# Loading q first and turning it one batch ahead in a fused attention and mixer kernel

## The chip, the core and the metric

The kernel runs on one core of a Trainium2 chip. A core has five engines that work side by side and wait for one another by semaphores: TensorE (PE; its weight loads, PEld, overlap its products), VectorE (DVE), ScalarE (ACT), GpSimd (POOL) and SyncE (SP). In this kernel SP only issues DMAs, and POOL issues the loads. Sixteen DMA engines move the data, and every queue shares them. The metric is device time of one execution in microseconds; lower is better.

## The reference

Eight batches go through an attention with a projected length of 64 for keys and values, and then through a mixer block. Cut to what is computed:

```python
k_proj = np.einsum('ks,bhsd->bhkd', E, k)      # 8 batches, 8 heads, S=1024, D=64, K=64
v_proj = np.einsum('ks,bhsd->bhkd', F, v)
attn = softmax(scale * q @ k_proj.T)           # over the 64 projected positions
x = (attn @ v_proj) as [8, 1024, 512]
h = np.maximum(x.T @ w_tok1, 0.0) @ w_tok2     # over the sequence, 1024 -> 256 -> 1024
u = x + h.T
out = u + np.maximum(u @ w_ch1, 0.0) @ w_ch2   # over the channels, 512 -> 1536 -> 512
```

Inputs and outputs are float32 in HBM. The kernel loads q, k, v and the weights as bf16 (the DMA converts), accumulates in float32 and stores float32.

## The kernel before

A batch has two halves. The **front** of batch b (`front`, L213) makes u: it projects k and v with `EFT` (`k_mm` L145, `v_mm` L150), turns the projected keys (`kt_step`), computes the scores of one head at a time (`score_step`, L177) and their exponentials (L182), multiplies by the projected v (`ou_step`, L190 to L197), and then does the two products over the sequence (L244, L256) and the sum u (L260). The **main part** of batch b is `up` (L388, 24 tiles of 4 products) and `down` (L441, a product of blocks in the manner of Strassen, with sums on DVE and POOL, and two stores of 512 KB for each half, L487 and L491).

The main part of batch b is interleaved with the front of batch b + 1 by hand. Both are generators that yield costs in microseconds; the loop at the end (L507 to L524) takes a step of the front whenever its due time has come. So each engine gets one fixed order of instructions, and an engine that waits holds up all that is behind it on that engine. Batch 0 has a front of its own, `front_first`, in pieces of two heads, sorted by a list `ev` of times written out by hand.

The scores need q with the head's dimension on the partitions. `load` (L82, issued by POOL) brings q, k and v of a batch as tiles `q_sb`, `k_sb` and `v_sb` of 1 MB. `turn_q` (L91, issued by SP) turns `q_sb` into `qT` with two crossbar transposes by DMA (L95), one for heads 0 to 3 and one for heads 4 to 7, 512 KB each. Each of these tiles has a single buffer. So the load of the next q waits until the turn of this q is done, the turn of the next q waits until the scores of this batch have read `qT`, and the next k and v wait for the projections of this batch. Batch 0 turns its q on PE instead.

In the kernel before, the turn of batch b is the first thing in front b, and the loads of batch b + 1 come behind the projections of front b, in the order k, v, q (`load_all`). On SP two other users stand in the same queue: the four crossbar transposes of u into `uT` at the end of a front (L262), which the next main part reads, and the stores of the output. On POOL the loads stand in one queue with three sums for each half of `down` (L475 to L477).

Of the kernel before, what the change touches and what calls it, by code (L numbers as in the profile page):

```python
# [16 lines left out]
def kernel(  # L17
# [15 lines left out]
    B, H, S, D = q.shape  # L33
# [52 lines left out]
    def load_all(b):  # L86
        load(b, "k", k)
        load(b, "v", v)
        load(b, "q", q)

    def turn_q(b):  # L91
        st["qT", b] = work.tile([P, H, 4, P], BF16, tag="qT", name="qT", bufs=1)
        for j in range(2):
            hs = slice(4 * j, 4 * j + 4)
            nc.sync.dma_start_transpose(  # L95
                out=st["qT", b][:, hs].rearrange("d h s p -> d (h s) p"),
                in_=st["q", b][:, hs].rearrange("p h x -> p (h x)"),
            )
# [24 lines left out]
    nc.gpsimd.dma_start(out=wt2, in_=moe_w_tok2.rearrange("(tc p) s -> p tc s", p=P))  # L123
    load_wc1(0)
    load_wc1(1)
    load_all(1)
    load_wc2(0)
    load_wc2(1)

# [74 lines left out]
    def new_front(b):  # L204
        st["x", b] = work.tile([P, SC, DM], BF16, tag="x_sb", name="x_sb", bufs=1)
        st["R", b] = work.tile([P, TC, DM], BF16, tag="R_sb", name="R_sb", bufs=1)
        st["u", b] = work.tile([P, SC, DM], BF16, tag="u_sb", name="u_sb", bufs=2)
        st["kp", b] = work.tile([KP, H, 2, D], BF16, tag="kprojs", name="kprojs", bufs=1)
# [4 lines left out]
    def front(b):  # L213

        al = slice(0, H)
        turn_q(b)
        new_front(b)
        kv_ps = front_ps("kv_ps")
        for si in range(SC):
            f = dict(start=(si == 0), stop=(si == SC - 1))  # L220
            k_mm(b, kv_ps, al, si, f)
            v_mm(b, kv_ps, al, si, f)
        k_out(b, kv_ps, al)
        if b + 1 < B:
            load_all(b + 1)
        yield 1.2
        v_out(b, kv_ps, al)
        yield 1.0
        kt_step(b, al, front_ps)
        yield 1.8  # L230
        score_step(b, 0, front_ps)
        yield 0.7
        score_step(b, 1, front_ps)
        yield 0.7
        for h in range(H):
            ou_step(b, h)
            yield 0.7
            if h + 2 < H:
                score_step(b, h + 2, front_ps)
                yield 0.5  # L240
        for t in range(TC):
            h_ps = front_ps("h_ps")
            for s in range(SC):
                nc.tensor.matmul(  # L244
                    h_ps, wt1[:, s, t * P : (t + 1) * P], st["x", b][:, s, :],
                    start=(s == 0), stop=(s == SC - 1),
                )
                if s % 2 == 1 and s < SC - 1:
                    yield 0.7
            nc.scalar.activation(out=st["R", b][:, t, :], in_=h_ps, func=ACT.Relu)  # L250
            yield 0.7 if t == 0 else 1.6
        new_uT(b)
        for s in range(SC):
            u_ps = front_ps("u_ps")
            for t in range(TC):
                nc.tensor.matmul(  # L256
                    u_ps, wt2[:, t, s::SC], st["R", b][:, t, :],
                    start=(t == 0), stop=(t == TC - 1),
                )
            nc.vector.tensor_add(out=st["u", b][:, s, :], in0=u_ps, in1=st["x", b][:, s, :])  # L260
            if s % 2 == 1:
                nc.sync.dma_start_transpose(  # L262
                    out=st["uT", b][:, s - 1 : s + 1].rearrange("d s c p -> d (s c) p"),
                    in_=st["u", b][:, s - 1 : s + 1].rearrange("p s d -> p (s d)"),
                )
            yield 0.9
# [7 lines left out]
    def front_first(fill):  # L274
        b = 0
        new_front(b)
        new_uT(b)
        st["qT", b] = work.tile([P, H, 4, P], BF16, tag="qT", name="qT", bufs=1)

        def q_turn(hp, psf):  # L280
            qt_ps = psf("qt_ps", BF16)
            for j in range(2):
                for s in range(4):
                    nc.tensor.transpose(
                        qt_ps[:, (j * 4 + s) * P : (j * 4 + s + 1) * P],
                        st["q", b][:, 2 * hp + j, s * P : (s + 1) * P], ident,
                    )
            nc.scalar.activation(
                out=st["qT", b][:, 2 * hp : 2 * hp + 2].rearrange("d h s p -> d (h s p)"),
                in_=qt_ps, func=ACT.Copy,  # L290
            )

        def proj(hp, psf, mm, fin):
            kv_ps = psf("kv_ps")
            hs = slice(2 * hp, 2 * hp + 2)
            for si in range(SC):
                mm(b, kv_ps, hs, si, dict(start=(si == 0), stop=(si == SC - 1)))
            fin(b, kv_ps, hs)

        def tok1(hp, psf):  # L300
            cs = slice(hp * P, (hp + 1) * P)
            h_ps = psf("h_ps")
            for t in range(TC):
                for s in range(SC):
                    nc.tensor.matmul(  # L305
                        h_ps[:, t * P : (t + 1) * P], wt1[:, s, t * P : (t + 1) * P],
                        st["x", b][:, s, cs], start=(s == 0), stop=(s == SC - 1),
                    )
            nc.scalar.activation(
                out=st["R", b][:, :, cs],  # L310
                in_=h_ps[:, 0 : TC * P].rearrange("p (t d) -> p t d", d=P), func=ACT.Relu,
            )

        def tok2(hp, psf, g):
            cs = slice(hp * P, (hp + 1) * P)
            u_ps = psf("u_ps")
            for i in range(4):
                for t in range(TC):
                    nc.tensor.matmul(
                        u_ps[:, i * P : (i + 1) * P], wt2[:, t, 4 * g + i :: SC],  # L320
                        st["R", b][:, t, cs], start=(t == 0), stop=(t == TC - 1),
                    )
            nc.vector.tensor_add(
                out=st["u", b][:, 4 * g : 4 * g + 4, cs],
                in0=u_ps.rearrange("p (s d) -> p s d", d=P),
                in1=st["x", b][:, 4 * g : 4 * g + 4, cs],
            )

        def turn_u(hp, psf):
            cs = slice(hp * P, (hp + 1) * P)  # L330
            ut_ps = psf("ut_ps", BF16)
            for s in range(SC):
                nc.tensor.transpose(ut_ps[:, s * P : (s + 1) * P], st["u", b][:, s, cs], ident)
            for g in range(2):
                o = st["uT", b][:, 4 * g : 4 * g + 4, hp, :]
                i_ = ut_ps[:, g * 512 : (g + 1) * 512].rearrange("d (s p) -> d s p", p=P)
                if g == 0:
                    nc.vector.tensor_copy(out=o, in_=i_)  # L338
                else:
                    nc.scalar.activation(out=o, in_=i_, func=ACT.Copy)  # L340

        ev = []
        t_q, t_k, t_v = (8.2, 12.0, 18.2, 21.9), (9.5, 13.2, 19.4, 23.1), (10.7, 14.4, 20.6, 24.4)
        t_w2 = 26.9
        for hp in range(HP):
            hs = slice(2 * hp, 2 * hp + 2)
            tk, tv, tq = t_k[hp], t_v[hp], t_q[hp]
            ev += [
                (tq, hp, lambda p, hp=hp: q_turn(hp, p)),
                (tk, hp, lambda p, hp=hp: proj(hp, p, k_mm, k_out)),  # L350
                (tk + 1.5, hp, lambda p, hs=hs: kt_step(b, hs, p)),
                (tv, hp, lambda p, hp=hp: proj(hp, p, v_mm, v_out)),
                (tk + 3.0, hp, lambda p, h=2 * hp: score_step(b, h, p)),
                (tk + 3.01, hp, lambda p, h=2 * hp + 1: score_step(b, h, p)),
            ]
            to = max(tv + 1.5, tk + 4.2)
            t1 = to + 2.6
            t2 = max(t1 + 1.7, t_w2 + 1.4 * hp)
            ev += [
                (to, hp, lambda p, h=2 * hp: ou_step(b, h)),  # L360
                (to + 1.1, hp, lambda p, h=2 * hp + 1: ou_step(b, h)),
                (t1, hp, lambda p, hp=hp: tok1(hp, p)),
                (t2, hp, lambda p, hp=hp: tok2(hp, p, 0)),
                (t2 + 0.5, hp, lambda p, hp=hp: tok2(hp, p, 1)),
                (t2 + 2.3, hp, lambda p, hp=hp: turn_u(hp, p)),
            ]
        ev += fill
        ev.sort(key=lambda e: e[0])
        pin = False
        for t, hp, fn in ev:  # L370
            pin = pin or hp is None
            fn(front_ps if pin else any_ps)
# [182 lines left out]
```

## Time and profile before

| | |
|---|---|
| median of three runs | 517.42 us (512.8 to 519.95) |
| the profiled execution | 514.69 us, of it span 512.9 us |
| granted TensorE clock, mean of the span | 0.953 |
| software DMA queue (loads) | 29.36 MB, 37.3% of 16 engines' span |
| hardware DMA queue (stores, crossbar) | 31.99 MB, 27.1% |

The profile is of one execution. Its page gives busy time for each engine, the span in 40 slices, the DMA queues, the chain of work that ended last, the costliest groups of instructions, and the DMA issues with their time from issue to landing. The trace behind it can be asked for waits, for a timeline, and for sums over stretches of time. An engine named with a q at its end, such as SPq, is the sequencer of that engine: it issues, waits and branches. The page's lines stand in the prediction where they are used.

### The profile page before, as it was taken

Reading aid. Unit: us, or ns where it says so; the run is one execution under the profiler, and the core shown is the slowest. Engines: PE = TensorE matmul, PEld = TensorE weight load, DVE = VectorE, ACT = ScalarE, POOL = GpSimd, SP = SyncE. Lnnn points to the kernel's source line nnn. Section 1 sums busy time; section 2 is a strip of 40 time slices with the busy share of each in tenths; the row PEclk is TensorE's granted clock in tenths of the full one; section 3 lists DMA queues with packets and bytes.
Section 4 is the critical chain, followed back from the end, with each engine's and each line's share of the span. In section 5 each row is a group of like instructions: output and inputs, shape, how many; then the busy total and the mean of one; then the engine's idle time right before and its main releaser. Section 6 shows DMA issues by size and latency. Waiting matters only on the chain.

```text
span 512.9 us, 7570 instructions
## 1 busy us (share of the span) xinstructions
PE 444.9 (87%) x3060; PEld 279.3 (54%) x3096; DVE 260.6 (51%) x527; ACT 187.1 (36%) x333; POOL 88.6 (17%) x95
## 2 busy tenths in 40 slices
PE   3789979975999759997699966999779999999996
PEld 2564356632486324863348633586335864487485
DVE  2374584553573525734457353474444747574453
ACT  3626731162502625025450263403544037502620
POOL 7320130300023000230002300024000220022022
PEclk9999989996999969998899997999879999999999
DMA  9999992897247981469914697056970661044003
GB/s 164 207 205 207 190 208 96 192 143 121 36 100 180 156 123 18 97 178 145 133 22 109 176 166 120 6 145 147 172 114 0 152 145 33 1 88 159 1 21 143
DMA packets 92690, 61.83 MB, mean 121 GB/s; under 512 B 59888, under 2 KB 88048, under 8 KB 92656
## 3 DMA queue, kind: packets, MB, share of 16 engines
q0 software_dynamic: 29200, 29.36, 37.3%
q1 hardware_dynamic: 63456, 31.99, 27.1%
q8 instruction: 24, 0.39, 0.3%
q14 instruction: 10, 0.08, 0.1%
HBM read 59.24 MB, written 16.78 MB: 148 GB/s over the span
## 4 chain that ended last, share of the span: by engine, by line
PE 67%; DMA 19%; DVE 7%; SPq 3%; ACT 2%; issue 1%; DVEq 0%; ACTq 0%
PE g_ps L388 22%; DMA qT<-q_sb 18%; PE be L441 12%; PE al L441 8%; PE ga L441 8%; PE h_ps L244 5%; PE u_ps L256 4%; DVE x_sb L197 4%; SPq L95 3%; PE ou_ps L190 3%; PE sco L177 2%; PE kv_ps L145 1%; DVE rdn L196 1%; DMA EF_f<-in_F_dram 1%; PE h_ps L305 1%
## 5 line engine op out<-in xcount | busy, mean ns | idle before, releaser
L388 PE MATMUL g_ps<-uT,wc 128*128 128x512 bf16 x768 | 198.5, 394 | 1.6 <-DVE uT L338 1.0
L420 ACT ACTIVATE g<-g_ps 128x512 bf16<-128x512 f32 x192 | 114.2, 597 | 132.7 <-PE g_ps L388 132.3
L388 PEld LDWEIGHTS <-wc 128*128 128x128 bf16 x768 | 74.4, 101 | 83.7 <-issue 16.0
L441 PEld LDWEIGHTS <-S 128*128 128x128 bf16 x768 | 75.3, 98 | 17.1 <-issue 0.3
L441 PEld LDWEIGHTS <-g 128*128 128x128 bf16 x576 | 56.6, 98 | 13.8 <-issue 0.3
L475 POOL TENSOR_TENSOR V<-V,u_sb 128x512 f32<-128x512 f32 x16 | 18.5, 1154 | 241.1 <-DVE V L470 241.1
L177 PE MATMUL sco<-qT,kbd 128*128 128x512 bf16 x48 | 20.8, 444 | 40.4 <-DMA qT<-q_sb 39.4
L182 ACT ACTIVATE attnT<-sco 128x512 bf16<-128x512 f32 x64 | 37.4, 594 | 47.4 <-PE sco L177 44.0
L190 PEld LDWEIGHTS <-attnT 128*128 128x128 bf16 x256 | 19.4, 103 | 62.6 <-issue 49.5
L196 DVE RECIPROCAL rdn<-ou_ps 128x8 f32<-128x8 f32 x64 | 13.2, 206 | 76.4 <-PE ou_ps L190 76.3
L441 PE MATMUL al<-wc,g 128*128 128x256 bf16 x384 | 50.4, 275 | 0.6
L441 PE MATMUL be<-dT,S 128*128 128x256 bf16 x384 | 48.8, 273 | 0.1
L197 DVE TENSOR_TENSOR x_sb<-ou_ps,rdn 128x512 bf16<-128x512 f32 x64 | 44.2, 691 | 2.2
L466 ACT ACTIVATE K<-al 128x512 f32<-128x512 f32 x16 | 9.6, 597 | 92.3 <-PE al L441 92.3
L260 DVE TENSOR_TENSOR u_sb<-u_ps,x_sb 128x512 bf16<-128x512 f32 x56 | 38.3, 685 | 6.6 <-PE u_ps L256 4.3
L406 DVE TENSOR_TENSOR S<-g 128x512 bf16<-128x512 bf16 x48 | 20.2, 421 | 31.5 <-ACT g L420 31.5
L190 PE MATMUL ou_ps<-vbd,attnT 128*128 128x130 bf16 x256 | 27.0, 232 | 9.6 <-DVE x_sb L197 7.4
L244 PE MATMUL h_ps<-x_sb,wt 128*128 128x512 bf16 x105 | 31.5, 379 | 1.7 <-DVE x_sb L197 1.3
L256 PE MATMUL u_ps<-R_sb,wt 128*128 128x512 bf16 x99 | 30.5, 379 | 0.0
L404 DVE TENSOR_TENSOR S<-g 128x512 bf16<-128x512 bf16 x48 | 20.2, 421 | 13.7 <-ACT g L420 13.5
L82 POOL DMA_DIRECT2D q_sb<-in_q_dram x11 | 9.2, 833 | 98.9 <-DMA qT<-q_sb 78.3
L441 PE MATMUL ga<-wc,S 128*128 128x256 bf16 x192 | 24.7, 273 | 0.0
(65 smaller groups left out, 395.5 us busy)
## 6 DMA issues: line engine op xcount, KB each, us to landing
out_dram<-o SPq DMA_DIRECT2D x32, 512.0 KB, 3.0
k_sb<-in_k_dram POOLq DMA_DIRECT2D x7, 1024.0 KB, 11.9
v_sb<-in_v_dram POOLq DMA_DIRECT2D x7, 1024.0 KB, 18.3
q_sb<-in_q_dram POOLq DMA_DIRECT2D x7, 1024.0 KB, 9.9
wc<-in_moe_w_ch_dram POOLq DMA_DIRECT2D x4, 384.0 KB, 13.9
wc<-in_moe_w_ch_dram POOLq DMA_DIRECT2D x2, 768.0 KB, 27.7
q_sb<-in_q_dram POOLq DMA_DIRECT2D x4, 256.0 KB, 8.7
k_sb<-in_k_dram POOLq DMA_DIRECT2D x4, 256.0 KB, 9.3
```

The source lines that it names most:

```text
L177: nc.tensor.matmul(sco, kbd[:, h, :], st["qT", b][:, h].rearrange("d s p -> d (s p)"), start=True, stop=True,)
L182: nc.scalar.activation(out=at, in_=sco, func=ACT.Exp, scale=scale)
L190: nc.tensor.matmul(ou[:, s // 2, o : o + 2 * D1], at[:, s * P : (s + 1) * P], vbd[:, h, :], start=True, stop=True,)
L197: nc.vector.tensor_tensor(out=st["x", b][:, :, h * D : (h + 1) * D].rearrange("p (b k) d -> p b k d", b=2), in0=ov[:, :, :, 0:D], in1=rdn[ ...
L244: nc.tensor.matmul(h_ps, wt1[:, s, t * P : (t + 1) * P], st["x", b][:, s, :], start=(s == 0), stop=(s == SC - 1),)
L256: nc.tensor.matmul(u_ps, wt2[:, t, s::SC], st["R", b][:, t, :], start=(t == 0), stop=(t == TC - 1),)
L260: nc.vector.tensor_add(out=st["u", b][:, s, :], in0=u_ps, in1=st["x", b][:, s, :])
L388: nc.tensor.matmul(st["g_ps", n], wc1[:, dc, cc * P : (cc + 1) * P], st["uT", b][:, 4 * sh : 4 * sh + 4, dc, :], start=(dc == 0), stop=(dc ...
L404: nc.vector.tensor_sub(out=s3, in0=a11, in1=a21)
L406: nc.vector.tensor_add(out=s1, in0=a21, in1=a22)
L420: nc.scalar.activation(out=o, in_=st["g_ps", n], func=ACT.Relu)
L441: nc.tensor.matmul(acc[:, e * HF : (e + 1) * HF], l[:, lc + c, l0 + (2 * j + e) * P : l0 + (2 * j + e + 1) * P], r[:, rc + c, r0 : r0 + HF ...
```

## The change

Two things move. First, the load of each q is issued ahead of the loads of its k and v. For batches 2 to 7 it stands at the beginning of the front of the batch before, ahead of that front's projections, while k and v stay behind them. Second, the turn of q of batch b + 1 is issued in front b, right behind the scores of head 7, and no longer at the beginning of front b + 1. For batch 1 it goes into `front_first`, behind the last scores of batch 0.

```diff
@@ the loads at the start
-    load_all(1)
+    load(1, "q", q)
+    load(1, "k", k)
+    load(1, "v", v)
...
@@ front(b)
-        turn_q(b)
         new_front(b)
+        if b + 1 < B:
+            load(b + 1, "q", q)
...
         k_out(b, kv_ps, al)
         if b + 1 < B:
-            load_all(b + 1)
+            load(b + 1, "k", k)
+            load(b + 1, "v", v)
...
             if h + 2 < H:
                 score_step(b, h + 2, front_ps)
+                if h + 2 == H - 1 and b + 1 < B:
+                    turn_q(b + 1)
                 yield 0.5
...
@@ front_first
+        ev.append((t_k[3] + 3.02, 3, lambda p: turn_q(1)))
         ev += fill
```

The order of the instructions on each engine shows it. PE, ACT and DVE have the same order in both kernels. Line numbers of the changed kernel are 6 or 7 higher behind the places of the edits.

SP before, from the turn of batch 1 to the first transposes of u of batch 2. The numbers tell buffers apart: `qT_704` and `qT_1177` are the turned q of batches 1 and 2, `uT_1038` and `uT_1527` those of u:

```order
L95 DMA_TRANSPOSE qT_704<-q_sb_111 128x16x128 x2
L487 DMA out_0_dram<-o1_823 128x1024
L491 DMA out_0_dram<-o2_824 128x1024
L262 DMA_TRANSPOSE uT_1038<-u_sb_709 128x8x128 x4
L487 DMA out_0_dram<-o1_1019 128x1024
L491 DMA out_0_dram<-o2_1020 128x1024
L95 DMA_TRANSPOSE qT_1177<-q_sb_734 128x16x128 x2
L262 DMA_TRANSPOSE uT_1527<-u_sb_1182 128x8x128 x3
```

SP in the changed kernel, the same stretch, where `qT_406`, `qT_929` and `qT_1398` belong to batches 1, 2 and 3:

```order
L95 DMA_TRANSPOSE qT_406<-q_sb_107 128x16x128 x2
L95 DMA_TRANSPOSE qT_929<-q_sb_711 128x16x128 x2
L494 DMA out_0_dram<-o1_823 128x1024
L498 DMA out_0_dram<-o2_824 128x1024
L268 DMA_TRANSPOSE uT_1041<-u_sb_709 128x8x128 x4
L494 DMA out_0_dram<-o1_1022 128x1024
L498 DMA out_0_dram<-o2_1023 128x1024
L95 DMA_TRANSPOSE qT_1398<-q_sb_1184 128x16x128 x2
L268 DMA_TRANSPOSE uT_1530<-u_sb_1182 128x8x128 x3
```

The turn of batch 2 moved ahead of two stores, of batch 1's four transposes of u, and of two more stores; each later turn moved likewise.

POOL before, from the loads of batch 1 to the sums of the first main part:

```order
L82 DMA k_sb_107<-in_k_dram 128x8x512
L82 DMA v_sb_109<-in_v_dram 128x8x512
L82 DMA q_sb_111<-in_q_dram 128x8x512
L113 DMA wc2_71<-in_moe_w_ch2_dram 128x6x512 x2
L82 DMA k_sb_730<-in_k_dram 128x8x512
L82 DMA v_sb_732<-in_v_dram 128x8x512
L82 DMA q_sb_734<-in_q_dram 128x8x512
L475 TENSOR_TENSOR V15_845<-V15_845,u_sb_138 128x512
```

POOL in the changed kernel, the same stretch:

```order
L82 DMA q_sb_107<-in_q_dram 128x8x512
L82 DMA k_sb_109<-in_k_dram 128x8x512
L82 DMA v_sb_111<-in_v_dram 128x8x512
L113 DMA wc2_71<-in_moe_w_ch2_dram 128x6x512 x2
L82 DMA q_sb_711<-in_q_dram 128x8x512
L82 DMA k_sb_732<-in_k_dram 128x8x512
L82 DMA v_sb_734<-in_v_dram 128x8x512
L482 TENSOR_TENSOR V15_845<-V15_845,u_sb_138 128x512
```

In each batch q stands ahead of k and v; the sums and the weights keep their places.

## The prediction

> **What bounds the kernel now.** I read the page first: the shares of the engines, the granted clock, the chain.
>
> ```profile
> span 512.9 us, 7570 instructions
> ...
> PE 444.9 (87%) x3060; PEld 279.3 (54%) x3096; DVE 260.6 (51%) x527; ACT 187.1 (36%) x333; POOL 88.6 (17%) x95
> ...
> PEclk9999989996999969998899997999879999999999
> ...
> PE g_ps L388 22%; DMA qT<-q_sb 18%; PE be L441 12%; PE al L441 8%; PE ga L441 8%; PE h_ps L244 5%; PE u_ps L256 4%; DVE x_sb L197 4%; SPq L95 3%; PE ou_ps L190 3%; PE sco L177 2%; PE kv_ps L145 1%; DVE rdn L196 1%; DMA EF_f<-in_F_dram 1%; PE h_ps L305 1%
> ```
>
> TensorE is busy 87% of the span, and the one thing beside it that holds a large share of the chain is the crossbar turn qT<-q_sb, 18%. The clock row has dips at places all over the span. The view of waits, PE alone (us in total, times, longest), says what PE stands still for:
>
> ```profile
> PE sco L177 <- DMA qT<-q_sb: 39.4, 7, 9.2
> PE e_ps L138 <- ACT EF_sb L134: 7.8, 1, 7.8
> ```
>
> Of the scores' waits for the turn there are seven, 39.4 us together; the next group is the single wait at the start. Whether these waits recur with the batches is read from the timeline of SP's queue (start, us spent issuing, line):
>
> ```profile
> 88.57 7.71 SPq L262 DMA_TRANSPOSE uT<-u_sb  x4
> ...
> 98.39 0.33 SPq L491 DMA_DIRECT2D out_dram<-o  x1
> ...
> 226.92 14.72 SPq L95 DMA_TRANSPOSE qT<-q_sb  x2
> ...
> 416.73 0.33 SPq L491 DMA_DIRECT2D out_dram<-o  x1
> 417.15 6.18 SPq L95 DMA_TRANSPOSE qT<-q_sb  x2
> 452.32 7.30 SPq L262 DMA_TRANSPOSE uT<-u_sb  x3
> ...
> 470.05 0.33 SPq L491 DMA_DIRECT2D out_dram<-o  x1
> ```
>
> The last store of a batch (L491) marks one period from the next. From 98.39 to 416.73 lie five periods, the fronts of batches 2 to 6: 318.34 us, 63.67 each. The sixth, front of batch 7, takes 470.05 - 416.73 = 53.32 us with the same instructions on PE, but without loads of k, v and q, for there is no batch 8. It is the pattern for a period in which the turn isn't disturbed. The windows compare the two, batch 3 and batch 7 from the start of the turn (us, busy per engine, granted clock, DMA share, GB/s):
>
> ```profile
> 162.74:176.00 13.26, 13.01 (x82) 5.87 (x81) 7.09 (x16) 9.76 (x18) 1.78 (x2) 1.00 1.11 190
> 176.00:184.86 8.86, 0.00 (x1) 0.00 (x0) 0.44 (x2) 0.60 (x1) 0.00 (x0) 0.67 1.10 148
> 184.86:190.00 5.14, 5.14 (x20) 2.32 (x20) 1.77 (x5) 2.13 (x4) 0.87 (x1) 0.58 0.59 74
> 417.15:430.41 13.26, 13.01 (x83) 5.88 (x81) 7.02 (x16) 9.77 (x18) 0.00 (x0) 1.00 0.67 131
> 380.00:512.90 132.90, 126.70 (x869) 83.07 (x876) 72.11 (x141) 46.68 (x82) 20.53 (x18) 1.00 0.29 77
> ```
>
> ```profile
> 184.86 0.59 PE L177 MATMUL sco<-qT,kbd 128*128 128x512 bf16 x1 [8.86 <-DMA qT<-q_sb]
> ...
> 430.32 0.38 PE L177 MATMUL sco<-qT,kbd 128*128 128x512 bf16 x1
> 435.29 0.10 PEld L177 LDWEIGHTS <-kbd 128*128 128x128 bf16 x1
> ```
>
> Up to the score of head 4 both take 13.26 us with PE busy 13.01: loads beside it don't slow PE. Then batch 3 waits 8.86 us for the second half of its turn, and batch 7 waits for nothing. Behind the wait the clock is 0.58 over 5.14 us in which PE is busy throughout, 5.14 x 0.42 = 2.2 us more. Why the turn is late is told by its landing (duration of the issue in ns; DMA to landing), in batch 3 and in batch 7:
>
> ```profile
> L95 SPq DMA_TRANSPOSE qT<-q_sb x1: 7935/7935/7935, 166.1 to 166.1; - x1
> DMA to landing us min/median/max: 18.7/18.7/18.7
> ...
> L95 SPq DMA_TRANSPOSE qT<-q_sb x1: 1967/1967/1967, 421.4 to 421.4; - x1
> DMA to landing us min/median/max: 4.4/4.4/4.4
> ```
>
> The same half of 512 KB takes 18.7 us beside the loads of k and v and 4.4 us alone.
>
> **The change part by part.** Nothing is added or removed: seven loads of q move ahead of k and v on POOL, and seven turns of two transposes each move to an earlier place on SP. PE, ACT and DVE keep their order.
>
> *The turn, batches 2 to 6.* It goes behind the last score of the batch before. In the pattern that score's weights load at 435.29, 18.1 us into the period, so SP issues about 18.7 in. It needs its q, and it would be slow if k and v were still coming:
>
> ```profile
> k_sb<-in_k_dram POOLq DMA_DIRECT2D x7, 1024.0 KB, 11.9
> v_sb<-in_v_dram POOLq DMA_DIRECT2D x7, 1024.0 KB, 18.3
> q_sb<-in_q_dram POOLq DMA_DIRECT2D x7, 1024.0 KB, 9.9
> ...
> 158.23 1.15 POOL L477 TENSOR_TENSOR K<-K,u_sb 128x512 f32<-128x512 f32 x1
> ...
> 165.37 0.91 POOL L82 DMA_DIRECT2D k_sb<-in_k_dram  x1 [5.99 <-PE kv_ps L150]
> ```
>
> The load of q has only to wait for POOL's add, whose end at 159.4 is 3.3 us ahead of the period's turn at 162.74; its own turn was done a period ago. At 9.9 us (the median, with nothing beside it but stores) it lands at 6.6. The loads of k and v are issued at 2.6 as before, and follow at 5.1 us each (the startup rows below), at about 17. So the turn at 18.7 finds q there and the DMA engines nearly free: issued within 6.2 us (row 417.15), landed 421.4 + 4.4 - 417.15 = 8.6 us later, at 27 of 53. The scores that need it come in the next period, more than 26 us on. Were the turn still disturbed, 18.7 us a half would also fit in. Price of the move: none; the five periods become like the sixth. That saves 318.34 - 5 x 53.32 = 51.7 us. Of it 39.4 are the waits, and the rest, 12.3 (2.5 a period), is the low clock behind them, as at 184.86.
>
> The Trainium skill (TensorE: Matmul & The Clock Gate, Part 1: The HAM clock gate) says that about 3.4 us of idle PE halves its clock, and about 3.4 us of activity restores it. By it one low window costs 1.7 us, so seven waits would cost at most 11.9 us, an estimate, and the sum would be 0.4 us higher. The trace has 1.00 where no wait lies, 380 to 512.9, so I keep the rows' 12.3.
>
> *What stands behind the turn on SP.* A turn that waits for a score or for q holds up what is queued behind it: the four transposes uT of the same batch and the two stores. In the pattern the first uT comes 452.32 - 417.15 = 35.2 us in and the turn leaves SP at 18.7 + 6.2 = 24.9; even the longest issue, 14.72 us at 226.92, ends at 33.4. Nothing waits: 0 us. Without that slack each microsecond would go to uT, and from there to the next batch's first products.
>
> *POOL.* If q has to wait for a turn, k and v now queue behind it. From batch 3 on it doesn't wait.
>
> *The startup, batch 1.* Here the loads form a backlog, and the turn falls into it:
>
> ```profile
> L82 POOL DMA_DIRECT2D k_sb<-in_k_dram x1: 884/884/884, 25.0 to 25.0; - x1
> DMA to landing us min/median/max: 15.0/15.0/15.0
> L82 POOL DMA_DIRECT2D v_sb<-in_v_dram x1: 873/873/873, 26.2 to 26.2; - x1
> DMA to landing us min/median/max: 18.9/18.9/18.9
> L113 POOL DMA_DIRECT2D wc<-in_moe_w_ch_dram x1: 826/826/826, 29.4 to 29.4; - x1
> DMA to landing us min/median/max: 29.4/29.4/29.4
> ...
> 54.92 0.40 PE L145 MATMUL kv_ps<-k_sb,EFT 128*64 128x512 bf16 x1
> ...
> 62.21 0.95 DVE L498 TENSOR_TENSOR dT<-wc,dT 128x1536 bf16<-128x1536 bf16 x1
> ...
> 68.44 0.15 PEld L177 LDWEIGHTS <-kbd 128*128 128x128 bf16 x1
> ```
>
> Loads landed in order, k at 40.0, v at 45.1, the last of wc2 at 58.8. Now q takes k's place and lands at 40.0, and the turn starts there. Beside a turn a load takes longer: v came 18.3 + 0.9 - 11.9 = 7.3 us behind k in the steady periods, against 5.1 here. So k lands by 47.3 and v by 54.6, just ahead of 54.92. The end of wc2 lies between 58.8 (no loss) and 58.8 + 5.1 = 63.9 (the turn's 1 MB at the pace of the loads); DVE reads it at 62.21, so it waits 0 to 1.7 us, and PE behind it. I take 0.9, the middle: both rows are equally near. The halves of the turn land by 40.0 + 18.7 = 58.7 and, the loads then ending, about 65, ahead of head 4 at 68.44. Load q of batch 2 waits for that, and k and v behind it come at about 82, needed at 98.8. Batch 2's turn, 5 us behind 68.44, meets them; by the 14.72 us of the longest issue SP is free at 88.1, and uT comes at 88.57.
>
> *Sum.* 512.9 - 51.7 + 0.9 = 462.1 us of span. The execution that was profiled took 514.69, 1.8 more than its span: 463.9 us. The median of the three runs, 517.42, stands 2.7 above that execution; the waits vary from run to run, so I expect the difference against the median to be somewhat larger.
>
> **The rivals.**
>
> *Only the waits go.* If the clock stays low for some other reason, 12.3 us stay: 476.2. Against it: 133 us at 1.00 in the window from 380 on, with PE busy 126.70. Chance 0.06.
>
> *The startup pays.* If the turn's second half lands behind 68.44, batch 1 gets the wait that batch 3 loses: 8.86 + 2.2 = 11.1 in place of 0.9, 474.1. For it: 18.7 us a half beside loads, two in a row from 40.0 would end at 77.4. Against it: the backlog ends by 63.9. The Trainium skill (DMA: Bandwidth & Descriptors, Queues, rings and completion order) has each DMA engine take the queues in turn, packet by packet, which is the rule against placing a turn in a backlog; 18.7 against 4.4 us agrees. Chance 0.06.
>
> *Slower.* The turn stands on SP ahead of the uT of its own front. Should q land more than 35.2 - 6.2 = 29 us into the period, each later microsecond is paid six times. To lose 2% over the 51.7 gained, q would have to be some 10 us later still, 42 us from issue: 463.9 + 6 x 10.3 = 526. Against it: 9.9 us to land, 18.3 at worst for v. Chance 0.02.
>
> *It does nothing.* The single buffers of q and qT chain load, turn and scores; if another such chain sets the period, the time stays at about 514. For it speaks no row; the sixth period shows none. Chance 0.03.
>
> **How the numbers follow.** The forecast has 0.83. Its low end is 0 for the startup and the 1.9 us by which the fastest run was below the profiled one: 461; I take 460. Its high end is 1.7 for the startup and the 5.3 us by which the slowest run was above it: 470.0; with half of the price of the startup's rival in, 472. The other cases, 0.17, stay outside. A measurement of this kernel tells about 2%, 10 us, from no change. Faster by more: the forecast and the first two rivals, 0.95; same 0.03; slower 0.02.
>
> **What would show it.** Right: no waits of the scores for the turn from batch 2 on; turns issued about 18.7 us into a period and landing within 9 us; periods of 53.3 us; clock 1.00 behind the startup. Wrong: SP still in a turn when u is ready, waits of up's products for uT, v of batch 1 behind 54.9, or a period above 55 with no idle PE.

## The result, and the profile after

| | before | changed |
|---|---|---|
| median of the runs | 517.53 us (4 runs, 512.8 to 519.95) | 472.71 us (4 runs, 471.46 to 473.26) |
| the profiled execution | 514.69 us, span 512.9 | 472.92 us, span 471.1 |
| granted TensorE clock | 0.953 | 0.984 |

The ratio is 0.914, with a 95% interval from 0.907 to 0.921. The kernel became faster by the mechanism that was forecast, but the time is 8.8 us above the forecast of 463.9, and 0.7 us above the range.

The changed kernel's page, span, TensorE, granted clock in 40 slices, and the chain:

```profile
span 471.1 us, 7571 instructions
...
PE 434.5 (92%) x3060; PEld 274.5 (58%) x3096; DVE 260.4 (55%) x527; ACT 186.3 (40%) x333; POOL 88.3 (19%) x95
...
PEclk9999989987999999999999999999999999999999
...
PE 85%; DVE 8%; DMA 3%; ACT 2%; issue 1%; SPq 0%; ACTq 0%; DVEq 0%
```

The chain is 85% TensorE, where the page before had 67%, and the transfers have 3% in place of 19%. The clock row is full from the eleventh slice on. The waits of TensorE in the changed kernel (us in total, times, longest):

```profile
PE e_ps L140 <- ACT EF_sb L136: 8.6, 1, 8.6
PE ou_ps L192 <- DVE x_sb L199: 7.4, 14, 2.2
PE g_ps L395 <- DMA uT<-u_sb: 6.7, 1, 6.7
```

All seven waits of the scores for the turn are gone. In their place stands one that the kernel before didn't have: a product of `up` waits 6.7 us, once, for a transpose uT. SP's timeline of the changed kernel tells in which period (start, us spent issuing, line):

```profile
74.73 12.77 SPq L95 DMA_TRANSPOSE qT<-q_sb  x2
...
99.22 0.33 SPq L498 DMA_DIRECT2D out_dram<-o  x1
127.88 4.15 SPq L95 DMA_TRANSPOSE qT<-q_sb  x2
...
162.02 0.47 SPq L498 DMA_DIRECT2D out_dram<-o  x1
181.13 4.55 SPq L95 DMA_TRANSPOSE qT<-q_sb  x2
...
428.28 0.33 SPq L498 DMA_DIRECT2D out_dram<-o  x1
```

From 162.02 to 428.28 lie five periods, the fronts of batches 3 to 7: 53.25 us each, and the forecast had 53.3. A turn is issued 181.13 - 162.02 = 19.1 us into its period (forecast 18.7), and the turns of batches 3 to 7 keep SP for 4.2 to 4.8 us each. But the period from 99.22 to 162.02, the front of batch 2, takes 62.80. That is 9.5 us more, and it is the whole difference from the forecast's span, 471.1 for 462.1. The windows of the changed kernel show how it divides (us, busy per engine, granted clock, DMA share, GB/s):

```profile
99.26:105.97 6.71, 0.00 (x1) 0.03 (x2) 0.00 (x0) 0.60 (x1) 0.00 (x0) 0.66 1.20 207
105.97:111.57 5.60, 5.60 (x21) 1.78 (x22) 0.00 (x0) 0.71 (x2) 0.00 (x0) 0.50 0.29 119
162.02:428.28 266.26, 261.48 (x1777) 162.73 (x1800) 156.76 (x315) 109.70 (x195) 43.73 (x41) 1.00 0.62 123
```

TensorE stands still for 6.71 us while the DMA engines are full, and then works 5.60 us at half the clock, 2.8 us lost. Two transposes, the third and the fourth of batch 1, have these landings in the changed kernel:

```profile
L268 SPq DMA_TRANSPOSE uT<-u_sb x1: 1231/1231/1231, 93.7 to 93.7; - x1
DMA to landing us min/median/max: 3.1/3.1/3.1
L268 SPq DMA_TRANSPOSE uT<-u_sb x1: 1320/1320/1320, 95.9 to 95.9; - x1
DMA to landing us min/median/max: 10.0/10.0/10.0
```

And POOL's timeline at that place:

```profile
93.36 1.16 POOL L484 TENSOR_TENSOR K<-K,u_sb 128x512 f32<-128x512 f32 x1
94.46 0.92 POOL L82 DMA_DIRECT2D q_sb<-in_q_dram  x1
111.68 0.87 POOL L82 DMA_DIRECT2D k_sb<-in_k_dram  x1 [16.30 <-PE kv_ps L152]
...
157.94 1.15 POOL L484 TENSOR_TENSOR K<-K,u_sb 128x512 f32<-128x512 f32 x1
159.03 0.91 POOL L82 DMA_DIRECT2D q_sb<-in_q_dram  x1
```

The load of q of batch 3 goes out at 94.46, as soon as POOL's last sum is done, and 1.4 us ahead of the issue of the fourth uT at 95.9. That transpose then lands in 10.0 us where its neighbour took 3.1. In the next period the load goes out at 159.03, and the last uT, issued at 153.0, has landed by then. Two causes are possible. Theory A: the load of q starves the last uT. Theory B: the turn of batch 2, which kept SP for 12.77 us from 74.73 on, beside the loads of k and v, has delayed the stores and uT behind it.

### The profile page after: what moved, and what is told of

Read it like the earlier page. It is cut to its first block, busy times and chain, and to the rows that moved or that the text cites. A ratio compares the mean times of both kernels' runs of the same rounds, so it can differ in the third digit from the quotient of the medians.

```text
span 471.1 us, 7571 instructions
## 1 busy us (share of the span) xinstructions
PE 434.5 (92%) x3060; PEld 274.5 (58%) x3096; DVE 260.4 (55%) x527; ACT 186.3 (40%) x333; POOL 88.3 (19%) x95
## 4 chain that ended last, share of the span: by engine, by line
PE 85%; DVE 8%; DMA 3%; ACT 2%; issue 1%; SPq 0%; ACTq 0%; DVEq 0%
PE g_ps L395 33%; PE be L448 13%; PE al L448 9%; PE ga L448 8%; PE h_ps L250 5%; PE u_ps L262 5%; DVE x_sb L199 4%; PE ou_ps L192 4%; PE kv_ps L147 3%; DMA uT<-u_sb 2%; PE sco L179 2%; DMA EF_f<-in_F_dram 1%; DVE rdn L198 1%; PE h_ps L311 1%; DVE u_sb L329 1%
## 5 line engine op out<-in xcount | busy, mean ns | idle before, releaser
L395 PE MATMUL g_ps<-uT,wc 128*128 128x512 bf16 x768 | 189.7, 381 | 8.3 <-DMA uT<-u_sb 6.7
L395 PEld LDWEIGHTS <-wc 128*128 128x128 bf16 x768 | 71.7, 98 | 85.5 <-issue 13.3
L192 PE MATMUL ou_ps<-vbd,attnT 128*128 128x130 bf16 x256 | 25.2, 221 | 10.0 <-DVE x_sb L199 7.4
L192 PEld LDWEIGHTS <-attnT 128*128 128x128 bf16 x256 | 17.4, 98 | 28.0 <-issue 14.2
L411 DVE TENSOR_TENSOR S<-g 128x512 bf16<-128x512 bf16 x48 | 20.2, 421 | 13.7 <-ACT g L427 13.5
L157 DVE CAST kprojs<-kv_ps 64x512 bf16<-64x512 f32 (+1 forms) x11 | 5.9, 536 | 39.2 <-ACT kprojs L156 39.2
L477 DVE TENSOR_TENSOR V<-ga,K 128x512 f32<-128x512 f32 x16 | 11.1, 691 | 25.7 <-PE ga L448 23.3
## 6 DMA issues: line engine op xcount, KB each, us to landing
q_sb<-in_q_dram POOLq DMA_DIRECT2D x7, 1024.0 KB, 13.5
```

The lines of the kernel that those rows point to most:

```text
L192: nc.tensor.matmul(ou[:, s // 2, o : o + 2 * D1], at[:, s * P : (s + 1) * P], vbd[:, h, :], start=True, stop=True,)
L395: nc.tensor.matmul(st["g_ps", n], wc1[:, dc, cc * P : (cc + 1) * P], st["uT", b][:, 4 * sh : 4 * sh + 4, dc, :], start=(dc == 0), stop=(dc ...
L411: nc.vector.tensor_sub(out=s3, in0=a11, in1=a21)
```

## The experiments

All are compared with the kernel before on the same chip. They ran on three chips, on which the kernel before had medians of 515.5 to 516.6 us, so times from different chips can differ by a microsecond for no other reason. A diff is against the changed kernel.

### e1 and e2: q behind the projections

```diff
 front(b)                                  # e1; e2 does it for b == 2 alone
-        if b + 1 < B:
-            load(b + 1, "q", q)
         kv_ps = front_ps("kv_ps")
...
         k_out(b, kv_ps, al)
         if b + 1 < B:
+            load(b + 1, "q", q)
             load(b + 1, "k", k)
```

> The load of q goes behind the projections of its front, still ahead of k and v; the turn stays early. Theory A (the load of q of batch 3 goes out 1.4 us ahead of the last transpose uT of batch 1 and starves it, which costs 6.7 us of wait and 2.8 us of low clock in one period): the wait of up's products for uT is gone, the period from 99 to 162 us becomes 53.3 like the others, the time is 472.7 - 9.5 = 463 us. Theory B (the turn of batch 2, kept on SP by the loads of k and v of batch 2 until 87.5 us, is what delays stores and uT): nothing changes there, 472 to 473 us.

> Only the load of q of batch 3 goes behind the projections of its front; all others stay as in the changed kernel. Theory A: 463 us, as much as when all are moved, since only this load meets a transpose of u. Theory B: 472 to 473 us.

Measured: 472.67 us (471.47 to 474.03, 6 runs) and 472.64 us (471.9 to 473.66, 6 runs). That looks like theory B, but the two kernels tell nothing. The line in the program moved behind the projections; the instruction on POOL did not. POOL does no part of the projections, so q stands on POOL in front of k as before, and nothing in front of it waits for TensorE. POOL's order is that of the changed kernel, row by row, and e1's timeline has the load at the old place:

```profile
93.13 1.17 POOL L483 TENSOR_TENSOR K<-K,u_sb 128x512 f32<-128x512 f32 x1
94.23 0.92 POOL L82 DMA_DIRECT2D q_sb<-in_q_dram  x1
```

They serve as two more measurements of the changed kernel: 472.6 to 472.7 three times.

### e3: the early turn alone

```diff
-    load(1, "q", q)
-    load(1, "k", k)
-    load(1, "v", v)
+    load_all(1)
 front(b)
-        if b + 1 < B:
-            load(b + 1, "q", q)
...
         if b + 1 < B:
-            load(b + 1, "k", k)
-            load(b + 1, "v", v)
+            load_all(b + 1)
```

> The turn is early as in the changed kernel, the loads have the order and the place of the kernel before (k, v, q). Theory A: q lands about 20 us into a period, some 1 to 2 us behind the last score, the turn is issued then, alone, and has left SP before uT; no load of q meets uT; 463 us. If q has to come first for the early turn to pay, the turn would come behind 35 us of a period and up's products would wait: above 475 us.

Measured: 462.18 us (461.64 to 462.54, 5 runs), ratio to the kernel before 0.896, interval 0.892 to 0.899. No wait of TensorE for a transpose by DMA is left. Loading q first is not needed for the early turn, and without it the kernel is 10.5 us faster than e1 and e2, which are the changed kernel on the same chip. Its median is the lowest of this study, though e4 and e5 lie within 1 us of it. It fits both theories: the load of q comes late here, but the turn of batch 2 also meets no loads.

### e4: the loads alone

```diff
 front(b)
+        turn_q(b)
         new_front(b)
...
-                if h + 2 == H - 1 and b + 1 < B:
-                    turn_q(b + 1)
...
-        ev.append((t_k[3] + 3.02, 3, lambda p: turn_q(1)))
```

> The loads have the order of the changed kernel, the turn stands at the beginning of its front as before. POOL holds k and v behind the load of q, and that waits for the turn, so the turn has the DMA engines to itself: first half landed about 6 us, second about 9 us into the period, needed at 6.3 and 13.2. If that is so the scores wait at most 0.5 us a period and the time is 463 to 466 us. If only the early turn removes the waits, the time stays at 510 to 518 us.

Measured: 463.05 us (461.93 to 464.32, 6 runs), ratio 0.897, interval 0.894 to 0.900. The turn stands where it stood in the kernel before, and the waits are gone all the same. e4's rows of SP and POOL at the front of batch 2 show why:

```profile
100.60 5.40 SPq L95 DMA_TRANSPOSE qT<-q_sb  x2
...
108.92 0.92 POOL L82 DMA_DIRECT2D q_sb<-in_q_dram  x1 [13.47 <-DMA qT<-q_sb]
109.82 0.89 POOL L82 DMA_DIRECT2D k_sb<-in_k_dram  x1
110.69 0.91 POOL L82 DMA_DIRECT2D v_sb<-in_v_dram  x1
```

The load of q waits for the turn, and k and v wait behind it in POOL's queue. So no load runs beside the turn, and it is issued within 5.4 us; in the kernel before the same turn, at 98.82, took 12.51. Either half of the change is enough; together they are slower than each alone.

### e5 and e6: theory A against theory B

In e5 the load of q of batch 3 alone stands behind a load that waits for the projections; the turns of batches 1 and 2 stay in their loads. In e6 it is the other way round: the turn of batch 2 meets no loads, and q of batch 3 stays in front.

```diff
 e5, front(b)
-        if b + 1 < B:
+        if b + 1 < B and b != 2:
             load(b + 1, "q", q)
...
             load(b + 1, "k", k)
+            if b == 2:
+                load(b + 1, "q", q)
             load(b + 1, "v", v)
 e6
-    load(1, "q", q)
-    load(1, "k", k)
-    load(1, "v", v)
+    load_all(1)
 front(b)
-        if b + 1 < B:
+        if b + 1 < B and b != 1:
             load(b + 1, "q", q)
...
             load(b + 1, "v", v)
+            if b == 1:
+                load(b + 1, "q", q)
```

> As the changed kernel, but in the front of batch 2 alone the load of q of batch 3 stands on POOL between the loads of k and v. The load of k waits for the projections of batch 2, so this q can't go out before them. The turns of batches 1 and 2 stay early and stay beside their loads. Theory A (the load of q of batch 3 starves the last transposes uT of batch 1): no wait of up's products for uT, 463 us. Theory B (the turn of batch 2, held on SP to 87.5 us by the loads of k and v of batch 2, delays the stores and uT): the wait of 7 us stays, 472 to 473 us.

> The other way round: loads of batches 1 and 2 in the old order (k, v, q), so the turn of batch 2 is alone and off SP by 83 us, but q of batch 3 stays ahead of its k and goes out right behind POOL's sums. Theory A: the wait of up's products for uT is there again, 6 to 7 us and the low clock behind it, 471 to 472 us. Theory B: no wait, 462 to 463 us.

Measured: e5 462.81 us (462.11 to 463.31, 4 runs), e6 472.51 us (471.35 to 472.65, 4 runs). The load of q of batch 3 and the landing of the fourth uT of batch 1, in e5 and in e6:

```profile
103.14 0.88 POOL L82 DMA_DIRECT2D q_sb<-in_q_dram  x1
...
L270 SPq DMA_TRANSPOSE uT<-u_sb x1: 1232/1232/1232, 95.8 to 95.8; - x1
DMA to landing us min/median/max: 3.0/3.0/3.0
```

```profile
93.31 0.91 POOL L82 DMA_DIRECT2D q_sb<-in_q_dram  x1
...
L268 SPq DMA_TRANSPOSE uT<-u_sb x1: 1374/1374/1374, 94.7 to 94.7; - x1
DMA to landing us min/median/max: 9.9/9.9/9.9
...
PE g_ps L395 <- DMA uT<-u_sb: 6.7, 1, 6.7
```

With q of batch 3 moved, and it alone, uT lands in 3.0 us and 9.7 us of time are gone (472.51 - 462.81, e6 and e5 on one chip). With the turn of batch 2 out of the loads and q of batch 3 left in front, uT takes 9.9 us, the wait is 6.7 us again, and the time is the changed kernel's. Theory B has fallen, and A has held from both sides.

How the transpose loses is in the view of the DMA queues (packets, MB, share of 16 engines in a stretch of 2 us). q0 is the queue of the loads, q1 that of SP. The rows are the changed kernel from 98 to 100 us, then from 102 to 104, and last e5 from 94 to 96, where no load runs:

```profile
q0 software_dynamic: 308, 0.32, 113.8%
...
q0 software_dynamic: 294, 0.30, 88.8%
q1 hardware_dynamic: 287, 0.07, 29.2%
...
q1 hardware_dynamic: 950, 0.24, 63.7%
```

From 98 to 100 us, with the transpose issued at 95.9, only the load's packets move. From 102 to 104 the two queues move about as many packets, 287 and 294, but a packet of the load carries about four times the bytes. With no load beside them the transposes move 950 packets in 2 us. Why the first stretch is the load's alone is not shown.

### e7: the meeting in further periods

```diff
 front(b)
-        if b + 1 < B:
+        if b == 1:
             load(b + 1, "q", q)
...
             nc.vector.tensor_add(out=st["u", b][:, s, :], in0=u_ps, in1=st["x", b][:, s, :])
+            if s == 6 and b + 2 < B:
+                mark = work.tile([P, 8], BF16, tag="mark", name="mark", bufs=1)
+                nc.gpsimd.tensor_copy(out=mark, in_=st["u", b][:, s, 0:8])
+                load(b + 2, "q", q)
```

> The changed kernel, but from the front of batch 2 on the load of the next q goes out earlier, behind a small copy on POOL that waits for the seventh of the eight sums u (the copy's tile is read by nobody). So in each period the load goes out about 1 to 1.5 us ahead of the last transpose uT, as it does in the changed kernel for batch 3 alone. Theory A (a load that starts ahead of the last uT starves it to about 10 us from issue to landing): the last uT lands about 163.5 in place of 158.9 in the period that ends at 162, where up's second tile needs it at 162.2, so 1 to 3 us of wait in each of the five periods that had none, and the 9.5 of the one that had it: 477 to 488 us. Theory C (the meeting hurts only in the crowded period of batch 1, behind the late turn and the startup's backlog): the last uT lands as before in the other periods, 471 to 474 us.

Measured: 493.95 us (493.42 to 495.49, 4 runs). Waits of e7 for uT, the landing of the last uT of batch 2 (the load of q went out ahead of it, at 152.8), and the two stores between which the four further periods lie:

```profile
PE g_ps L399 <- DMA uT<-u_sb: 21.1, 5, 7.4
...
L272 SPq DMA_TRANSPOSE uT<-u_sb x1: 2026/2026/2026, 153.4 to 153.4; - x1
DMA to landing us min/median/max: 11.9/11.9/11.9
...
162.44 0.33 SPq L502 DMA_DIRECT2D out_dram<-o  x1
...
397.59 0.33 SPq L502 DMA_DIRECT2D out_dram<-o  x1
```

Four more periods met the load (the edit reaches the fronts of batches 1 to 5), not five as I had written, and each paid; the time lies above theory A's 477 to 488 all the same. The old wait is 7.4 of the 21.1 us, so the four have 13.7, 3.4 each, somewhat over the expected 1 to 3. The four periods last 397.59 - 162.44 = 235.15 us, 22.1 more than four of 53.25, 5.5 each, for behind a wait of 3 to 4 us the clock drops as well, which the expectation left out. The crowded period of batch 1 is no condition: theory C has fallen. That the other periods of the changed kernel go unharmed is a matter of place: in the first of them the load of q starts at 159.03, and the last uT, issued at 153.0, lands in 5.9 us, at 158.9.

## Why the prediction was right in kind and too low by 9 us

- *The bound and the saving.* Right. The 39.4 us of waits and the low clock behind them were the price of a turn beside loads, and the period of batch 7 was the right pattern: 53.25 us against 53.32.
- *The turn on SP.* Right: issued 19.1 us into a period, landed in 4.3 to 6.1 us a half, off SP long before uT. Two terms beside it were too low, at no cost: the load of q at 159.03 took 13.5 us, not 9.9, and v landed at 183.5, 21.5 us into its period and not 17, so the turn at 181.1 still met the end of v. With more than 26 us to spare that did not matter. The rival in which the turn holds up uT didn't come. Nor did the one in which the clock stays low.
- *The startup.* Its term was 0.9 us and measured nothing. The store that ends the startup comes 0.83 us later than before (99.22 for 98.39), and that is the size by which the first wait of TensorE, for the inputs E and F, came out longer in this execution, 8.6 for 7.8 us (7.4 to 9.5 over the profiled executions). The second half of batch 1's turn was in time for its scores.
- *The step that failed* is the price of the move in "the turn, batches 2 to 6": "Price of the move: none; the five periods become like the sixth." I had asked what the moved turn would hold up on SP, and what the moved load of q would wait for on POOL. I had not asked what the load would meet on the DMA engines when it goes out earlier. Its place was taken from a period in which POOL's last sum ends behind the last uT, and the sentence said that beside it were only stores. In the period of batch 2's front POOL's last sum is done at 94.5 and the last uT is issued at 95.9. Four of the five periods came out as forecast, and the one of batch 2's front cost 9.5 us: 6.7 of wait for the uT that the load held up, 2.8 of low clock. The rows of the kernel before had both times: SP's four uT were issued from 88.57 over 7.71 us, to 96.3, and POOL's last sum was done at 93.7, by this row:

```profile
92.52 1.16 POOL L477 TENSOR_TENSOR K<-K,u_sb 128x512 f32<-128x512 f32 x1
```

- *The size could have been estimated from a row that the prediction used.* A 512 KB half of the turn took 18.7 us beside loads and 4.4 alone. The same ratio turns the 3.0 us of a uT into 13; it took 10.0, and of the 6.9 us more than its neighbour's TensorE waited 6.7. With the measured 9.5 us in it the sum is 473.4, 0.7 us from the median.
- *The range.* Its upper end, 472, does not follow from its words: half of the startup rival's 11.1 us in place of the 1.7 gives 473.9, and 472 is half of the way from 470.0 to 474.1. The wider end would have taken the measured time in, by luck: that room was meant for the startup, which cost nothing.
- *Which part of the change did it.* Not both together, as the forecast had it: e3 and e4 show that the early turn alone, or the order of the loads alone, removes the same waits. Only both together leave the load of q with nothing to wait for on POOL, and so let it out ahead of the last uT.

## What to carry to other kernels

When a load is moved earlier, look up every transfer that is in flight at its new place, in each period of the kernel and not in a typical one, and which of them somebody waits for. A crossbar transpose on the critical path should have no bulk load start ahead of it; a load can be held back by putting it behind another one that waits for the right thing on the same queue. And when an experiment moves a line of a program, look at the order on the engine that issues it: a line behind the projections is not an instruction behind them.

## What the runs showed of the hardware

- A load that starts just ahead of a crossbar transpose slows the transpose far more than it is slowed itself. 256 KB landed 3.0 to 3.1 us after issue in the period of batch 2's front with no load issued ahead of it (e5, and the third uT of the changed kernel, 0.7 us ahead of the load), 3.9 to 5.9 us in the changed kernel's later periods, right behind two stores, and 9.9 to 12.9 us when a load of 1 MB had gone out 0.4 to 1.4 us ahead of it (changed kernel, e6, e7). The load itself took 10.7 us there (changed kernel, 94.5 to 105.2), where the loads of q in the steady periods of the kernel before took 9.2 to 10.0.
- A stop of TensorE of only 3 us is paid again in clock. The windows of e7 at such a wait:

```profile
162.47:165.47 3.00, 0.00 (x1) 0.03 (x1) 0.00 (x0) 0.60 (x1) 0.00 (x0) 1.00 1.16 278
165.47:169.10 3.63, 3.63 (x14) 1.29 (x16) 0.00 (x0) 0.60 (x1) 0.00 (x0) 0.53 0.39 159
```

The Trainium skill (TensorE: Matmul & The Clock Gate, Part 1: The HAM clock gate) says that the clock halves after about 3.4 us without work. Here 3.00 us were enough, and the clock was low for about as long afterwards. So the four waits of e7, 13.7 us, cost 22.1.
